# Expert-choice routing: the first expert's token numbers by four broadcast comparisons and one f16 number a token, with its gathers and its products moved forward in the written order

## The chip, the cores and the metric

One NeuronCore of one Trainium2 chip runs the whole program as one launch. It has five engines with a queue of instructions each: TensorE (PE, with its weight loads as PEld), VectorE (DVE), ScalarE (ACT), GpSimd (POOL) and SyncE (SP, which only issues DMAs here). An engine takes its instructions in the order of its queue; a wait holds all that stands behind it. The metric is the device time of one execution in microseconds; a profiled execution also gives a span, from the first to the last instruction.

## The reference

Three stages in f32, each on the output of the one before:

- Attention, 4 batches x 8 heads x 768 positions x 64: a position sees `n_sink` first positions and a window of `window` positions back; softmax; then the product with v.
- A dense layer on the 3072 x 512 result: `h = x @ w_in` (2048 wide), a smooth ReLU (0 below -1, (h+1)^2/4 between, h above 1), `@ w_out`.
- Expert choice among 8 experts of 384 places each:

```python
order = np.argsort(-flat)                      # all token x expert logits, largest first
for idx in order:
    tok, e = (int(idx) // E, int(idx) % E)
    if assigned[tok] >= 0 or counts[e] >= cap:
        continue
    assigned[tok] = e
    counts[e] += 1
...
for e in range(E):
    mask = assigned == e
    h = np.maximum(x[mask] @ w1[e], 0.0)       # 512 -> 1024
    out[mask] = h @ w2[e]                      # 1024 -> 512
```

## The kernel before, in words

Products are done in about f32 precision: each operand is split into a high and a low part ("h" and "l"), and a product is three matmuls, (low weights, high data), (high, low), (high, high).

The first 790 us hold attention and the dense layer, block by block of 256 tokens; the last block's logits are made before the rest of that block's output products (`up`, L663), so that the search for the first expert runs beside them. `logits` (L680) copies the logits from PSUM on ACT and turns them.

The routing is done expert by expert in the order in which experts fill up. `phase` (L789) holds the steps for one expert, the 3072 tokens lying as 128 partitions x 24 columns (GT = 24):

- `values`, `owners`: the best remaining logit of each token and its expert. Then seven rounds of a search for the threshold at which an expert is full: `compare` (DVE, 128 x 768), `count` and `total` (PE), `counts` and `bound` (DVE).
- `above`, `loads`, `choose`, `before`, `rank`: which expert is full, and the rank of each of its tokens (1 to 384). `choose` gives SP the expert's number for its weight loads.
- `places`: `a` (L943, L944), the place 1 to 128 of each token within a third of the expert's 384, and `rr` (L945), on POOL, which holds partition number and column number of a token, each in the column of its third.
- `slots(h)`, for h in 0 to 3: one-hot tiles `oh`, a comparison of the row 1 to 128 (`nrow`) with `a[:, t]` for each of the six columns t of a quarter: 24 DVE instructions of 128 x 128 in all (L958). `look(h)`: six matmuls with `oh` as weights and `rr` as data sum the numbers into `pk` in PSUM (L962). For the first expert a filler matmul (`unread`, L782), whose result nobody reads, follows each.
- `tokens`: ACT copies half of `pk` to SBUF (`tf`, L968), DVE makes 128 x column + partition of both halves, the token numbers `tok` (L972).
- `retire` (L926): five DVE operations that take the expert and its tokens out of the logits. The next expert's `values` need them.

`gather` (L1018) issues on POOL three indirect DMAs of 128 rows each by `tok` (L1025). `turn` (L1031): PE turns such a tile (`xt`, L1039), ACT copies it as the high part (`xsh`, L1040), DVE makes the low part (`xsl`, L1043). `expert` (L1047): for f = 0 to 7, `up` (12 matmuls into one of two PSUM buffers "H", which the fillers use as well), `act` (ACT) and `rest` (DVE, `hl`, L1076); from f = 3 on, `down` steps. `weight` (L977) brings the weights in eight pieces of 512 KB. A piece is loaded by SP into one of four buffers "er". For w2, and for the first piece of w1 of the first expert, ACT writes minus the weights (`minus`, L1000) and the high part (`lead`, L1006), and POOL issues a DMA that adds the weights to make the low part (`add`, L1010); for the other w1 pieces DVE makes the low part in two halves (`rest`, L1014). The first expert's other six pieces wait for its gathers (L992).

`experts` (L1121) writes all this into a plan: each step gets a time, and the steps of each engine are issued in the order of these times. `start` is the end of the logits. `T[k]` is the planned start of the products of expert k, `g` that of its three turns. The second expert's search is planned at `start + FIND + SECOND`, each later one at least `CHAIN` after the one before, and the T of each expert at least one of `PERIODS` after that of the one before. Steps given as `filler` are moved into planned gaps of DVE.

The planned times that the change touches, in us after `start`, before and after it:

| step (first expert, but for the search of the second) | before | after |
|---|---|---|
| `slots` 0 to 3 | 29.0, 29.6, 30.2, 30.8 | 29.0, 29.4, 29.8, 30.2 |
| `tokens` / `gather` / `retire` | 32.6 / 32.7 / 31.4 | 30.75 / 30.8 / 30.85 |
| `values` of the second search | 32.8 | 31.4 |
| `add` of the first w1 and the first w2 piece | 30.2, 40.8 | 31.8, 33.8 |
| `xt` 0 to 2 | 37.9, 39.2, 40.5 | 34.9, 36.23, 37.56 |
| `xsl` 0 to 2 | 39.35, 40.4, 42.15 | 36.1, 37.43, 38.76 |
| second search: `compare` 1, `count` 1, `total` 1 | 37.65, 38.65, 39.5 | 36.25, 37.25, 38.1 |
| second search: `bound` 1, `compare` 2, `count` 2 | 40.2, 41.1, 42.1 | 38.8, 39.7, 40.7 |
| loads of the other six weight pieces, from | 38.4 | 34.4 |
| T[0], first product | 42.8 | 38.8 |
| second low half of the second w1 piece / `compare` 3 | 46.25 / 44.55 | 44.2 / 43.15 |
| third part of the products of f = 1 / `up` f = 2, first part | 46.91 / 47.74 | 42.91 / 43.74 |
| third search: `count` 0 | 70.65 | 69.25 |
| T[1], T[2], T[3], T[4] | 82.3, 121.8, 161.3, 200.8 | 78.3, 117.8, 158.55, 198.05 |

Of the kernel before, what the change touches and what calls it, by code (L numbers as in the profile page):

```python
# [7 lines left out]
F32 = mybir.dt.float32  # L8
# [17 lines left out]
P = 128  # L26
# [33 lines left out]
SECOND, CHAIN, EARLY = 11.3, 34.8, 59.0  # L60
# [14 lines left out]
class Kernel:  # L75
# [547 lines left out]
    def moe1_steps(self, blk, xs, hold=None, part=None):  # L623
# [56 lines left out]
        def logits():  # L680
            lg = self.mo.tile([2 * E, TB], F32, name="lgs", tag="u")
            nc.scalar.copy(lg, st["lg"])
            ps = self.psum([P, 2, 2 * E], "A", "lt")
            for t in range(2):
                nc.tensor.transpose(ps[:, t], lg[:, t * P:(t + 1) * P], self.ident[:2 * E, :2 * E])
            o = self.logits[:, 2 * blk:2 * blk + 2, :]
            nc.vector.tensor_copy(o, ps[:, :, :E])
            nc.vector.tensor_tensor(out=o, in0=o, in1=ps[:, :, E:], op=OP.add)
# [47 lines left out]
    def pools2(self, e):  # L736
        tc = self.tc
        self.oh = e(tc.tile_pool(name="oh", bufs=1))
        self.ex = e(tc.tile_pool(name="ex", bufs=2))
        self.ew = e(tc.tile_pool(name="ew", bufs=2))  # L740

    def router_consts(self):
# [8 lines left out]
        self.nrow = rt.tile([P, P], BF16, name="nrow")  # L751
# [15 lines left out]
        self.t_row = rt.tile([P, GT], F32, name="t_row")  # L767
        nc.vector.tensor_copy(self.t_row, fl[:, 0, :GT])
# [20 lines left out]
    def phase(self, last, out, first=False):  # L789
# [147 lines left out]
        def places():  # L937
# [6 lines left out]
            nc.vector.scalar_tensor_tensor(a, a, -float(P), z, op0=OP.mult, op1=OP.add)  # L944
            rr = st["rr"] = self.rw.tile([P, GT, 2, 3], BF16, name="rr")  # L945

            nc.gpsimd.tensor_scalar(rr[:, :, 0].rearrange("p t c -> p c t"), bs, self.pcol, None, op0=OP.mult)
            nc.gpsimd.tensor_tensor(out=rr[:, :, 1].rearrange("p t c -> p c t"), in0=bs,
                                    in1=self.t_row.unsqueeze(1).to_broadcast([P, 3, GT]), op=OP.mult)
            st["oh"] = self.oh.tile([P, GT, P], BF16, name="oh", bufs=1)  # L950
            st["a"] = a
            st["pk"] = self.psum([P, 6], "A", "pk")
# [3 lines left out]
        def slots(h):  # L956
            for t in range(n_ * h, n_ * h + n_):
                nc.vector.tensor_scalar(st["oh"][:, t], self.nrow, st["a"][:, t:t + 1], None, op0=OP.is_equal)  # L958

        def look(h):  # L960
            for t in range(n_ * h, n_ * h + n_):
                nc.tensor.matmul(st["pk"], st["oh"][:, t], st["rr"][:, t].rearrange("p x c -> p (x c)"),  # L962
                                 start=(t == 0), stop=(t == GT - 1))
                if first and t < GT - 1:
                    self.unread(1, 5 * 32)
            if h == NQ - 1:
                st["tf"] = self.rw.tile([P, 3], F32, name="tf")
                nc.scalar.copy(st["tf"], st["pk"][:, 0:3])  # L968

        def tokens():  # L970
            out["tok"] = self.rw.tile([P, 3], I32, name="tok", bufs=3)
            nc.vector.scalar_tensor_tensor(out["tok"], st["pk"][:, 3:6], float(P), st["tf"], op0=OP.mult, op1=OP.add)  # L972
# [74 lines left out]
    def expert(self, cur):  # L1047
# [6 lines left out]
        def up(f):  # L1054
# [5 lines left out]
            def part(i):  # L1060
                w_, x_ = ((wl, xh), (wh, xl), (wh, xh))[i]
# [59 lines left out]
    def experts(self, plan, start):  # L1121
# [41 lines left out]
        for k in range(E):  # L1163
# [21 lines left out]
            if k == 0:  # L1185
                for dt, n in ((4.3, 10), (11.6, 8), (15.4, 4), (16.9, 2), (18.2, 2), (20.1, 3)):
# [4 lines left out]
            if k < 3:  # L1191

                for h in range(NQ):
                    at(t, ph["slots"], h)
                    at(t + 0.7, ph["look"], h)
                    t += 0.6
# [22 lines left out]
            for j in range(3):  # L1219
# [7 lines left out]
                filler(g + step * j + 1.2, 0.8, lambda tr=tr: tr["f"][1]())  # L1227
# [4 lines left out]
            for i, (c, name) in enumerate(PIECES):  # L1232
# [11 lines left out]
                if dma:  # L1244
# [3 lines left out]
                    at(a1 + 1.1 if k or i != 2 else T[0] - 2.0, add)  # L1248
# [5 lines left out]
            steps, ups, ends, act, rest = self.expert(cur)  # L1254
# [268 lines left out]
```

## Time and profile before

| | us |
|---|---|
| three timed runs | 1159.52 (median), 1156.93, 1160.38 |
| the profiled execution: its time, its span | 1156.74, 1154.9 |
| busy in the span: PE, PEld | 1101.7 (95%), 1014.5 (88%) |
| busy in the span: DVE, ACT, POOL | 872.7 (76%), 698.5 (60%), 487.2 (42%) |
| mean granted TensorE clock | 0.992 of 2.4 GHz |

A share of busy time is an average over stages. The stretch around the change lies between 814 us (end of the first search) and 835 us (first product of the first expert); from there to 1148 us the products of eight experts follow on PE. In a timeline each row is one or several like instructions: start, time from the start of the first to the end of the last, engine, line, operation, tiles, and in brackets how long the engine had been idle before it and what ended that.

### The profile page before, as it was taken

How to read it: one execution, taken by the hardware profiler on the slowest of the kernel's cores; microseconds unless marked ns; L12 is line 12 of the kernel's file. 1: busy time of each engine (PE TensorE's matmuls, PEld its weight loads, DVE VectorE, ACT ScalarE, POOL GpSimd, SP SyncE). 2: the span in 40 equal slices, each digit the busy share in tenths (PEclk: the TensorE clock that was granted, in tenths of full speed). 3: DMA queues.
4: the chain of work that ended last, by engine and by line, in shares of the span. 5: the costliest groups of instructions: out<-in, count | busy, mean ns of one | idle time of the engine just before them, and what ended most of it. 6: DMA issues, size and time to landing. Idle time of an engine off the chain costs nothing.

```text
span 1154.9 us, 24467 instructions
## 1 busy us (share of the span) xinstructions
PE 1101.7 (95%) x8308; PEld 1014.5 (88%) x8308; DVE 872.7 (76%) x2718; ACT 698.5 (60%) x1598; POOL 487.2 (42%) x590
## 2 busy tenths in 40 slices
PE   5899888999999999999999999999899999999997
PEld 3688878999999999999999999999678788888896
DVE  5978978777878878787878787755888888889430
ACT  4887777566777666776767676642245435444552
POOL 1335645445654545555545555541212323332321
PEclk9899999999999999999999999999999999999999
DMA  4645522222322223223222322000576767676872
GB/s 106 169 137 169 164 60 56 54 60 45 69 47 54 38 54 53 65 47 65 35 54 50 70 49 52 15 19 1 152 210 181 218 178 207 179 205 197 227 212 67
DMA packets 241928, 118.13 MB, mean 102 GB/s; under 512 B 196096, under 2 KB 220672, under 8 KB 241792
## 3 DMA queue, kind: packets, MB, share of 16 engines
q1 hardware_dynamic: 231504, 85.36, 28.7%
q0 software_dynamic: 8592, 29.89, 11.0%
q8 instruction: 67, 1.10, 0.4%
q10 hardware_dynamic: 1696, 1.22, 0.3%
q14 instruction: 69, 0.57, 0.2%
HBM read 86.00 MB, written 13.11 MB: 86 GB/s over the span
## 4 chain that ended last, share of the span: by engine, by line
PE 54%; DVE 13%; issue 7%; ACT 4%; POOL 3%; DMA 3%; SPq 1%; POOLq 0%; DVEq 0%; ACTq 0%
PE hp L638 17%; PE up L663 16%; PE us L1090 6%; PE hp L1063 6%; PE xp L391 3%; DVE ks L301 2%; PE tp L372 2%; PE sc L334 2%; PE sc L335 1%; DVE oh L958 1%; DVE ind L814 1%; DVE u L646 1%; PE pg L829 1%; DVE ql L317 1%; DVE w1l L1014 1%
## 5 line engine op out<-in xcount | busy, mean ns | idle before, releaser
L650 POOL TENSOR_TENSOR gl<-u,gh 128x256 fp32r<-128x256 f32 x192 | 153.2, 798 | 187.3 <-ACT gh L649 163.3
L663 PE MATMUL up<-woh,gl 128*128 128x256 f32 x576 | 166.5, 289 | 2.6 <-POOL gl L650 2.6
L663 PE MATMUL up<-woh,gh 128*128 128x256 f32 x576 | 163.8, 284 | 0.0
L663 PE MATMUL up<-wol,gh 128*128 128x256 f32 x576 | 163.5, 284 | 0.0
L647 ACT ACTIVATE u<-u,half 128x256 f32<-128x256 f32 x192 | 97.4, 508 | 79.3 <-DVE u L646 74.9
L638 PE MATMUL hp<-xh,wil 128*128 128x256 f32 x768 | 131.1, 290 | 4.0 <-ACT xh L411 3.2
L638 PE MATMUL hp<-xl,wih 128*128 128x256 f32 x768 | 125.8, 284 | 1.3 <-POOL xl L412 1.1
L638 PE MATMUL hp<-xh,wih 128*128 128x256 f32 x768 | 124.4, 283 | 0.0
L638 PEld LDWEIGHTS hp<-xh,wil 128*128 128x128 f32 x768 | 106.7, 190 | 5.9 <-ACT xh L411 4.3
L663 PEld LDWEIGHTS up<-woh,gl 128*128 128x128 f32 x576 | 108.9, 189 | 3.1 <-POOL gl L650 3.1
L663 PEld LDWEIGHTS up<-wol,gh 128*128 128x128 f32 x576 | 108.6, 188 | 0.4 <-issue 0.4
L663 PEld LDWEIGHTS up<-woh,gh 128*128 128x128 f32 x576 | 108.5, 188 | 0.4 <-issue 0.4
L638 PEld LDWEIGHTS hp<-xl,wih 128*128 128x128 f32 x768 | 106.1, 190 | 2.5 <-POOL xl L412 2.5
L638 PEld LDWEIGHTS hp<-xh,wih 128*128 128x128 f32 x768 | 106.1, 191 | 0.0
L646 DVE TENSOR_SCALAR u<-hp 128x256 f32<-128x256 f32 x192 | 80.1, 417 | 32.2 <-PE hp L638 24.4
L648 DVE TENSOR_TENSOR u<-hp,u 128x256 f32<-128x256 f32 x192 | 80.4, 419 | 31.4 <-ACT u L647 29.3
L649 ACT CAST gh<-u 128x256 fp32r<-128x256 f32 x192 | 77.5, 404 | 29.6 <-DVE u L648 26.9
L353 POOL TENSOR_TENSOR pr<-pr,sm 128x576 f32<-128x576 f32 x56 | 65.6, 1171 | 68.3 <-DVE ks L307 31.6
L339 ACT ACTIVATE pr<-pr,sm 128x288 f32<-128x288 f32 (+1 forms) x160 | 85.2, 533 | 12.6 <-DVE sm L337 11.7
L1071 ACT ACTIVATE hh<-hp 128x384 fp32r<-128x384 f32 x64 | 31.5, 492 | 100.6 <-PE hp L1063 86.4
L1090 PE MATMUL us<-w2h,hl 128*128 128x512 f32 x192 | 80.8, 421 | 0.0
L1090 PE MATMUL us<-w2h,hh 128*128 128x512 f32 x192 | 75.6, 394 | 0.0
(266 smaller groups left out, 3018.8 us busy)
## 6 DMA issues: line engine op xcount, KB each, us to landing
w1r<-in_moe_w_dram SPq DMA_DIRECT2D x32, 512.0 KB, 4.8
w2r<-in_moe_w_dram SPq DMA_DIRECT2D x32, 512.0 KB, 3.9
w2l<-w2r POOLq DMA_DIRECT2D x32, 512.0 KB
qr<-in_q_dram SPq DMA_DIRECT2D x320, 32.0 KB, 2.0
dr<-in_moe_w_in_dram SPq DMA_DIRECT2D x15, 512.0 KB, 3.9
dr<-in_moe_w_out_dram SPq DMA_DIRECT2D x15, 512.0 KB, 3.9
x2d<-ev SPq DMA_DIRECT2D x26, 256.0 KB, 2.5
vr<-in_v_dram SPq DMA_DIRECT2D x56, 96.0 KB, 2.4
```

Of the source, the lines that this page charges most:

```text
L339: nc.scalar.activation(pr, pr, AF.Exp, bias=sm[:, 0, u:u + 1], scale=-1.0, accum_out=sm[:, 1, u:u + 1])
L353: nc.gpsimd.tensor_tensor(out=pr, in0=pr, in1=r.unsqueeze(2).to_broadcast([P, 2, 2 * P + NS]), op=OP.mult)
L391: nc.tensor.matmul(o_, l, r, start=(i == 0), stop=(i == len(mm) - 1), skip_group_check=True)
L638: nc.tensor.matmul(ps, w_[:, k, fs], x_[:, k, :], start=(i == 0 and k == 0), stop=(i == 2 and k == 3))
L646: nc.vector.tensor_scalar(u, ps, -1.0, 1.0, op0=OP.max, op1=OP.min)
L647: nc.scalar.activation(u, u, AF.Square, bias=self.half, scale=0.5)
L648: nc.vector.tensor_tensor(out=u, in0=ps, in1=u, op=OP.max)
L649: nc.scalar.copy(gh, u)
L650: nc.gpsimd.tensor_tensor(out=gl, in0=u, in1=gh.bitcast(F32), op=OP.subtract)
L663: nc.tensor.matmul(o, g_[:, ts], self.w_out_part(w_, f)[:, cs], start=(f == fa and i == 0 and (cs.start > 0 or t == 0)), stop=(f == fz - 1 ...
L1063: nc.tensor.matmul(ps, w_[:, k, fs], x_[:, k, :], start=(i == 0 and k == 0), stop=(i == 2 and k == 3))
L1090: nc.tensor.matmul(us[j], h_[:, o], w_[:, f % 2, :], start=(f == 0 and i == 0), stop=(f == nf - 1 and i == 2))
```

## The change

Four things. First, for the first expert the one-hot tiles are made with the token column innermost: four DVE operations of 128 x 128 x 6, each comparing a stored f16 tile `slot` (the row 1 to 128 repeated 24 times, written once by four ACT copies queued behind the copy of the logits) with a broadcast of `a` in f16. The weights of `look` are then read from `oh` at a step of 24 elements. One filler of 512 columns follows each of the first three `look` steps, in place of 23 fillers of 160 columns. Second, for all experts `rr` holds one f16 number a token, its number minus 1536: one POOL operation in place of two, three result columns in place of six, no ACT copy, and `tokens` reads PSUM. Third, `tokens` and `gather` of the first expert come before `retire`, and the two DMAs that add weights behind the gathers. Fourth, the plan: times as in the table above, and the three parts of the first four `up` of the first expert in the order (high, high), (low, high), (high, low).

```diff
-SECOND, CHAIN, EARLY = 11.3, 34.8, 59.0
+SECOND, CHAIN, EARLY = 9.9, 34.8, 59.0
+XT, LEAD = 34.9, 38.8
...
-            nc.scalar.copy(lg, st["lg"])
+            self.copied = nc.scalar.copy(lg, st["lg"]).ins
...
+        self.slot = self.oh.tile([P, P, GT], F16, name="slot", bufs=1)
+        with tc.issue_after(self.copied):
+            for i in range(0, P, 32):
+                self.nc.scalar.copy(self.slot[:, i:i + 32],
+                                    self.nrow[:, i:i + 32].unsqueeze(2).to_broadcast([P, 32, GT]))
...
-        self.nrow = rt.tile([P, P], BF16, name="nrow")
+        self.nrow = rt.tile([P, P], F16, name="nrow")
...
-        self.t_row = rt.tile([P, GT], F32, name="t_row")
-        nc.vector.tensor_copy(self.t_row, fl[:, 0, :GT])
+        self.tok = rt.tile([P, GT], F32, name="tok_row")
+        nc.vector.tensor_scalar(self.tok, fl[:, 0, :GT], float(P), self.pcol, op0=OP.mult, op1=OP.add)
+        nc.vector.tensor_scalar(self.tok, self.tok, float(-N // 2), None, op0=OP.add)
...
-            rr = st["rr"] = self.rw.tile([P, GT, 2, 3], BF16, name="rr")
-
-            nc.gpsimd.tensor_scalar(rr[:, :, 0].rearrange("p t c -> p c t"), bs, self.pcol, None, op0=OP.mult)
-            nc.gpsimd.tensor_tensor(out=rr[:, :, 1].rearrange("p t c -> p c t"), in0=bs,
-                                    in1=self.t_row.unsqueeze(1).to_broadcast([P, 3, GT]), op=OP.mult)
-            st["oh"] = self.oh.tile([P, GT, P], BF16, name="oh", bufs=1)
-            st["a"] = a
-            st["pk"] = self.psum([P, 6], "A", "pk")
+            at = st["a"] = self.rw.tile([P, GT], F16, name="ah") if first else a
+            nc.vector.scalar_tensor_tensor(at, a, -float(P), z, op0=OP.mult, op1=OP.add)
+            rr = st["rr"] = self.rw.tile([P, GT, 3], F16, name="rr")
+            nc.gpsimd.tensor_tensor(out=rr.rearrange("p t c -> p c t"), in0=bs,
+                                    in1=self.tok.unsqueeze(1).to_broadcast([P, 3, GT]), op=OP.mult)
+            st["oh"] = self.oh.tile([P, P, GT] if first else [P, GT, P], F16, name="oh", bufs=1)
+            st["pk"] = self.psum([P, 3], "A", "pk")
...
+            ts = slice(n_ * h, n_ * h + n_)
+            if first:
+                nc.vector.tensor_tensor(out=st["oh"][:, :, ts], in0=self.slot[:, :, ts],
+                                        in1=st["a"][:, ts].unsqueeze(1).to_broadcast([P, P, n_]), op=OP.is_equal)
+                return
...
-                nc.tensor.matmul(st["pk"], st["oh"][:, t], st["rr"][:, t].rearrange("p x c -> p (x c)"),
+                nc.tensor.matmul(st["pk"], st["oh"][:, :, t] if first else st["oh"][:, t], st["rr"][:, t],
                                  start=(t == 0), stop=(t == GT - 1))
-                if first and t < GT - 1:
-                    self.unread(1, 5 * 32)
-            if h == NQ - 1:
-                st["tf"] = self.rw.tile([P, 3], F32, name="tf")
-                nc.scalar.copy(st["tf"], st["pk"][:, 0:3])
+            if first and h < NQ - 1:
+                self.unread(1)
...
-            nc.vector.scalar_tensor_tensor(out["tok"], st["pk"][:, 3:6], float(P), st["tf"], op0=OP.mult, op1=OP.add)
+            nc.vector.tensor_scalar(out["tok"], st["pk"], float(N // 2), None, op0=OP.add)
...
-                w_, x_ = ((wl, xh), (wh, xl), (wh, xh))[i]
+                w_, x_ = ((wl, xh), (wh, xl), (wh, xh))[(i + 2) % 3 if lead and f < 4 else i]
...
-                for dt, n in ((4.3, 10), (11.6, 8), (15.4, 4), (16.9, 2), (18.2, 2), (20.1, 3)):
+                for dt, n in ((4.3, 10), (9.4, 8), (13.1, 3), (14.5, 2), (15.0, 2), (16.8, 2)):
...
-                at(t, ph["retire"])
-                at(t + 1.2, ph["tokens"])
-                at(t + 1.3, self.gather, cur)
-                t += 1.3
-                g, step = t + 5.2, 1.3
-                T.append(max(T[-1] + PERIODS[k - 1], g + 4.9) if k else g + 4.9)
+                if k:
...
+                else:
+                    at(t + 0.15, ph["tokens"])
+                    at(t + 0.2, self.gather, cur)
+                    at(t + 0.25, ph["retire"])
+                    g, step = start + XT, 1.33
+                    T.append(start + LEAD)
...
-                filler(g + step * j + 1.2, 0.8, lambda tr=tr: tr["f"][1]())
+                if k:
+                    filler(g + step * j + 1.2, 0.8, lambda tr=tr: tr["f"][1]())
+                else:
+                    at(g + step * j + 1.2, lambda tr=tr: tr["f"][1]())
...
-                    at(a1 + 1.1 if k or i != 2 else T[0] - 2.0, add)
+                    at(a1 + 1.1 if k else max(a1 + 1.1, T[0] - 7.0 + i), add)
```

## Rows read from the trace of the kernel before

**Rows 1.** Busy by stage: stretch, length, each engine's busy time, PEclk, DMA share.

```profile
834.57:877.65 43.08, 41.60 (x293) 33.70 (x290) 36.52 (x143) 19.76 (x28) 9.99 (x11) 1.00 0.75 214
877.00:917.00 40.00, 39.35 (x279) 31.75 (x278) 33.74 (x135) 17.39 (x26) 9.15 (x12) 1.00 0.69 190
```

**Rows 2.** Timeline of PE: start, length, engine, line, operation, idle before.

```profile
829.90 0.63 PE L1039 MATMUL xt<-ident,xg 128*128 128x128 f32 x4 [1.01 <-issue]
...
832.43 0.63 PE L1039 MATMUL xt<-ident,xg 128*128 128x128 f32 x4 [0.27 <-DVE row L853]
...
834.57 0.94 PE L1063 MATMUL hp<-xsh,w1l 128*128 128x384 f32 x4
...
839.52 0.85 PE L1063 MATMUL hp<-xsh,w1l 128*128 128x384 f32 x4
840.22 0.86 PE L1063 MATMUL hp<-xsl,w1h 128*128 128x384 f32 x4
...
861.68 0.33 PE L962 MATMUL pk<-rr,oh 128*128 128x6 bf16 x6
```

**Rows 3.** Timeline of DVE.

```profile
820.20 4.38 DVE L958 TENSOR_SCALAR oh<-nrow,a 128x128 bf16<-128x128 bf16 x24
...
825.40 0.15 DVE L972 SCALAR_TENSOR_TENSOR tok<-pk,tf 128x3 int32<-128x3 f32 x1
...
829.55 0.96 DVE L814 TENSOR_TENSOR ind<-v,th 128x768 bf16<-128x768 f32 x1
...
840.40 0.96 DVE L814 TENSOR_TENSOR ind<-v,th 128x768 bf16<-128x768 f32 x1
```

**Rows 4.** Timeline of POOL.

```profile
823.76 1.13 POOL L1010 DMA_DIRECT2D w1l<-w1r  x1 [2.91 <-PE idle L787]
825.85 1.07 POOL L1025 DMA_INDIRECT xg<-x2d,tok  x1 [0.96 <-DVE tok L972]
...
828.51 0.95 POOL L1025 DMA_INDIRECT xg<-x2d,tok  x1 [0.30 <-issue]
829.47 1.04 POOL L1010 DMA_DIRECT2D w2l<-w2r  x1
```

**Rows 5.** Timeline of ACT.

```profile
817.24 0.37 ACT L710 COPY ev<-up 128x256 f32<-128x256 f32 x1 [24.74 <-PE up L663]
...
833.10 0.59 ACT L1040 CAST xsh<-xt 128x512 fp32r<-128x512 f32 x1 [0.84 <-PE xt L1039]
836.64 1.05 ACT L1006 CAST w1h<-w1r 128x1024 fp32r<-128x1024 f32 x1 [2.96 <-DMA w1r<-in_moe_w_dram]
```

**Rows 6.** Timeline of SP, which only issues DMAs.

```profile
832.49 1.12 SPq L991 DMA_DIRECT2D w1r<-in_moe_w_dram  x2
...
835.34 0.37 SPq L991 DMA_DIRECT2D w1r<-in_moe_w_dram  x1
```

**Rows 7.** DVE groups by form, 790 to 1155 us: count, busy us, mean ns of one.

```profile
L814 DVE TENSOR_TENSOR ind<-v,th 128x768 bf16<-128x768 f32 x35 | 33.5, 956 | 0.9
...
L877 DVE TENSOR_REDUCE ce<-w 128x8 bf16<-128x192 bf16 x8 | 4.0, 503 | 0.3
...
L804 DVE TENSOR_TENSOR own<-logits,v 128x192 bf16<-128x192 f32 x8 | 2.8, 352 | 0.1
...
L895 DVE TENSOR_TENSOR w<-own,est 128x192 bf16<-128x192 bf16 x8 | 2.1, 258 | 0.0
```

**Rows 8.** Weight loads of PE by form, the whole run: count, busy us, mean ns.

```profile
L1063 PEld LDWEIGHTS hp<-xsh,w1h 128*128 128x128 f32 x256 | 43.8, 188 | 0.1
L372 PEld LDWEIGHTS tp<-ident,pr 128*128 128x128 f32 x296 | 41.6, 207 | 3.7 <-POOL pr L353 3.5
...
L962 PEld LDWEIGHTS <-oh 128*128 128x128 bf16 x192 | 9.3, 96 | 8.5 <-DVE oh L958 3.2 <-issue 1.8 <-PE idle L787 1.0
```

**Rows 9.** Busy by stage, early in the attention.

```profile
28.00:32.00 4.00, 2.30 (x15) 1.64 (x13) 3.77 (x17) 3.92 (x13) 2.60 (x5) 1.00 0.27 52
32.00:44.00 12.00, 11.50 (x51) 9.28 (x52) 11.77 (x39) 8.88 (x26) 5.47 (x9) 0.72 0.61 163
```

More of the change, by code (lines that the diff above doesn't have):

```diff
@@ L943, in places @@
             nc.vector.tensor_tensor(out=a, in0=ge[:, 1], in1=ge[:, 2], op=OP.add)
-            nc.vector.scalar_tensor_tensor(a, a, -float(P), z, op0=OP.mult, op1=OP.add)
-            rr = st["rr"] = self.rw.tile([P, GT, 2, 3], BF16, name="rr")
-            nc.gpsimd.tensor_scalar(rr[:, :, 0].rearrange("p t c -> p c t"), bs, self.pcol, None, op0=OP.mult)
-            nc.gpsimd.tensor_tensor(out=rr[:, :, 1].rearrange("p t c -> p c t"), in0=bs,
-                                    in1=self.t_row.unsqueeze(1).to_broadcast([P, 3, GT]), op=OP.mult)
-            st["oh"] = self.oh.tile([P, GT, P], BF16, name="oh", bufs=1)
-            st["a"] = a
-            st["pk"] = self.psum([P, 6], "A", "pk")
+            at = st["a"] = self.rw.tile([P, GT], F16, name="ah") if first else a
[5 more added lines that the diff above has]
+            st["pk"] = self.psum([P, 3], "A", "pk")
         n_ = GT // NQ
         def slots(h):
-            for t in range(n_ * h, n_ * h + n_):
+            ts = slice(n_ * h, n_ * h + n_)
[3 more added lines that the diff above has]
+                return
+            for t in range(ts.start, ts.stop):
                 nc.vector.tensor_scalar(st["oh"][:, t], self.nrow, st["a"][:, t:t + 1], None, op0=OP.is_equal)
@@ L1045, in turn, with expert @@
         return turned, rest
-    def expert(self, cur):
+    def expert(self, cur, lead):
         nc, a, tc = self.nc, self.a, self.tc
@@ L1194, in experts @@
                     at(t, ph["slots"], h)
-                    at(t + 0.7, ph["look"], h)
-                    t += 0.6
-                at(t, ph["retire"])
-                at(t + 1.2, ph["tokens"])
-                at(t + 1.3, self.gather, cur)
-                t += 1.3
-                g, step = t + 5.2, 1.3
-                T.append(max(T[-1] + PERIODS[k - 1], g + 4.9) if k else g + 4.9)
+                    at(t + (0.7 if k else 0.5), ph["look"], h)
+                    t += 0.6 if k else 0.4
+                if k:
+                    at(t, ph["retire"])
+                    at(t + 1.2, ph["tokens"])
+                    at(t + 1.3, self.gather, cur)
+                    t += 1.3
+                    g, step = t + 5.2, 1.3
+                    T.append(max(T[-1] + PERIODS[k - 1], g + 4.9))
+                else:
[4 more added lines that the diff above has]
+                    T.append(start + LEAD)
                 if T[k] - 6.2 > g:
@@ L1252, in experts @@
                         filler(a1 + 1.2 + 0.7 * u, 2.5, rest, u)
-            steps, ups, ends, act, rest = self.expert(cur)
+            steps, ups, ends, act, rest = self.expert(cur, k == 0)
             d = PERIODS[k] / len(steps)
```

## The prediction

> **What bounds the kernel now.** I read the stages first, to see which engine sets the time behind the change. From the first product of the first expert (834.57 us) to that of the second (877.65 us) PE is busy 41.60 of 43.08 us, and 39.35 of 40.00 us in the next stage [rows 1]. So behind 834.57 us PE is the bound, and a product that starts earlier carries through to the end, as long as nothing that PE waits for stays where it was. Ahead of it PE waits for one chain, read from the timelines of the engines: DVE makes 24 one-hot tiles from 820.20 to 824.58, the token numbers come at 825.40, after the logits' update [rows 3], POOL issues gathers from 825.85 to 829.46 [rows 4], PE turns the tiles from 829.90 to 832.43 and starts products at 834.57 [rows 2]. Last I read, for the weights of the first expert, SP [rows 6] and ACT [rows 5]: their loads leave at 832.49, behind the last gather, and the cast of the second w1 piece runs at 836.64.
>
> **The one-hot tiles.** Removed: 24 operations, 4.38 us. Added: four of 128 x 768 with 16-bit operands; none stands in the trace. With an f32 operand the same size takes 956 ns, and 192 elements take 352, so an element costs (956 - 352) / 576 = 1.05 ns. With 16-bit operands alone 192 elements take 258, 94 less, which is about half of 192 x 1.05: half an element's time is saved [rows 7]. For 768 that gives 956 - 400 = 556 ns. Here the elements come in rows of six with a hop between; a reduction that hops at each of 192 elements takes 503, 151 more than the operation of 352, or 0.8 ns a hop [rows 7], so 128 hops add 0.1: 0.66. In a queue the next one starts before the last is out; I take 0.56 a piece and 0.66 for the last: 820.2 + 3 x 0.56 + 0.66 = 822.5. Ends: 0.46 a piece, 822.1; at full length (0.87 a piece), 823.8.
>
> **The look-up and the numbers.** Six matmuls of the last quarter follow. With contiguous weights six took 0.33 [rows 2]; I take 0.43, because the weights now lie 48 bytes apart. The ACT copy and the logits' update no longer stand in between, so DVE makes the numbers at 822.5 + 0.43 = 822.95, against 825.40: 2.45 earlier. The lower end is 0.33. The upper end: a 16-bit load takes 96 ns, an f32 load 188, and an f32 load in steps of two 207 [rows 8]; at 0.207 each, six take 1.24, four such quarters with three fillers (about 0.2 each) become longer than the DVE work, and the numbers come at 820.7 + 4 x 1.24 + 0.7 = 826.4. The nearest row by type is the 96. Against it speaks a rule of the Trainium skill (Advanced Engine Details and Errata, Memory Cachelines): full rate needs two hits on a 16-byte line, and here each column is on a line of its own. No run here shows 16-bit weights so spaced; the same skill (TensorE: Matmul & The Clock Gate, Weight-path perf modes) lets the fast weight load read strided columns, which would leave 0.33.
>
> `rr` as one POOL operation, and the missing ACT copy, cost or save nothing: POOL and ACT are idle there, and `rr` is used only after the first one-hot. The ACT fill of `slot`, four copies of 768 elements, is some 3.4 us by the 1.05 of 1024 [rows 5]; ACT is idle for 24.74 us before 817.24 [rows 5], which hides it. Without that cover (fill behind the copies at 817.24) the tiles would start at about 822, 1.7 later.
>
> **The gathers.** POOL starts 0.30 after the numbers (825.55 to 825.85): 823.4. The third starts 2.66 behind the first (825.85 to 828.51) [rows 4]: 826.05. The first tile landed 4.05 after its start (829.90) and the third 3.95 after (turned at 832.43, SP free at 832.49) [rows 2, 6]: now 827.45 and 830.0. The DMA that adds to w1 stood ahead of the gathers at 823.76 [rows 4] and now stands behind; a quicker landing by that I leave to the range.
>
> **Turns and the first product.** The update now follows the numbers and takes about 1 us (824.58 to 825.40 is its visible part), so the second search starts near 824.2, 1.3 earlier; its `compare` 1, at 829.55 before, could run at 828.2. But in the new order `xsl` 0 stands ahead of it on DVE and waits for the first tile: turned at 827.45, cast 0.67 later for 0.59 (832.43 to 833.10 and on) [rows 2, 5], 828.7; `xsl` of 512 elements by 352 + 320 x 1.05 is 0.69, of which 0.6 blocks DVE: 829.3. `compare` 1 ends at 830.25, `count` 1 takes 0.15, and behind it on PE stands the third turn: 830.4. Its tile is cast at 830.4 + 0.67 + 0.59 = 831.65, and the first product, which with the new order of parts needs only the high halves, starts there: 2.9 earlier than 834.57. The plan's 4.0 is not reached.
>
> **What is late next.** (a) The second part needs the first w1 piece's low half. Its adding DMA is now issued after the third gather, 827.0. How long one takes is read from the w2 one: issued at 829.47, and SP's load at 835.34, which reuses the buffer that it reads, waits for it: 5.9 [rows 4, 6]. It is there at 832.9, and the part wants it at 832.35: 0.5 lost, 0 to 2.6 for a DMA of 4 to 8 us. (b) The loads behind the gathers go at 830.0, not 832.49; the second w1 piece is cast 4.15 after (832.49 to 836.64) for 1.05: 835.2. From there DVE took until 840.40, 2.7 us after the cast's end at 837.69, for a low half, `hl` 0, the other low half and a `bound`, and then began `compare` 4 [rows 3, 5]. The new order puts a `compare`, 0.96, in between before the second half is made: 835.2 + 2.7 + 0.96 = 838.85. The products of f = 2 need both halves from their second part on, which ran at 840.22 [rows 2]. So there the gain is down to 1.4. Below, it would be nothing if the weights came no earlier; above, 2.9 if DVE kept ahead.
>
> **Until the second expert.** PE idles 43.08 - 41.60 = 1.48 us in this stage [rows 1], at `count` steps that come before DVE is ready. Products stand 4.0 earlier in the plan and the search 1.4, so each count comes 2.6 later behind the products; I take 1.0 of the 1.48 as regained (ends 0 and 1.48). At the second expert the gain is 2.4. After it PE idles 0.65 in 40 us, the third search starts no earlier than before, and the plan gives T[3] only 2.75 of the 4.0: I take off 0.3 (0 to 1.0). Forecast: 2.1 us less.
>
> **The sum.** 1156.74 for the profiled execution less 2.1 is 1154.6. That execution is 0.2 below the fastest of the three timed ones; all four have a mean of 1158.4, which I use as the level: 1156.3.
>
> **Rivals.**
> - Most of the shift passes: one-hot pieces at 0.46, tiles landing 0.5 sooner without the adding DMA ahead, DVE ahead of the products. The product starts at 830.9, no loss at f = 2, and the plan's 2.75 at T[3] with the lost waits gives 3.2 to 3.7: 1155.0. For it: DVE idle while the tiles fly. Against: the weights leave only after the gathers.
> - Weight loads at the 48-byte step are slow. From 0.17 us a load on, four quarters are longer than the old chain to 825.40; at 0.207 the numbers come 1.0 later than before, everything behind moves with them, and the earlier counts return nothing: slower, 1159.5. For it: the 207 row. Against: that row's loads move four-byte elements, whose contiguous load is 188 already. The rule of the Trainium skill on lines (Memory Cachelines, above) is this case's mechanism.
> - The clock falls. After a stretch in which PE was busy 2.30 of 4.00 us the granted clock was 0.72 on average over 12 us, between 2.4 and 1.2 GHz: 0.28 x 12 = 3.4 us of work lost [rows 9]. Fillers here are rearranged, and by my times PE is busy some 60% from 823 to 831.6. If the products start at 1.2 GHz: 1156.3 + 3.4 = 1159.7. Against it: the stage that follows ran at 1.00 before [rows 1] with waits as long.
> - It doesn't do what it says: `slot` is filled late, or the adding DMA takes 8 us; 1.7 or 2.1 of the gain are lost: 1158.2.
>
> **How the numbers follow.** Forecast 0.45; most passes 0.20; slow loads 0.10; clock 0.08; late fill or late DMA 0.17. The forecast's own range, by its bounds and a level uncertain by 1.5, is 1154.3 to 1158.3. The range over the cases is 1152.7 to 1159.9. A measurement of this kernel tells 0.3%, 3.5 us, from no change. Faster by more needs the second case and luck, or the first with much luck: 0.27. Slower by more needs slow loads or the clock and something else: 0.09. Within: 0.64.
>
> **What would show it.** Right: four DVE rows `oh` of some 0.65 us, ending by 822.6; the numbers before 823.2; the third turn held by `count` 1, not by its tile; the first product near 831.7; PE idle ahead of the second part, and again at f = 2 for a `w1l`; the second expert's first product about 2.4 earlier. Wrong: `oh` rows of 0.9, `pk` steps longer than the `oh` rows, PEclk under 1.00 from 825 on, or a PE stall at the `count` 0 of the third or fourth search that takes the gain back.

## The result, and the profile after: slower by 0.8%

The changed kernel takes 1167.58 us (median of 6 runs, 1163.96 to 1168.64), the kernel before in the same comparison 1158.35 (6 runs, 1156.44 to 1160.38): ratio 1.0076, 95% interval 1.0065 to 1.0088. I forecast 1156.3 in a range up to 1159.9. The profiled execution took 1167.97 us (span 1166.2), 11.23 more than the one before. Of that 1.07 had arisen ahead of anything that the change touches: the copy of the last block's logits, `lgs`, starts at 793.20 us instead of 792.13. Runs of kernels that are the same up to there differ by as much (791.5 to 794.2), so below I count from that copy.

Busy by stage, from the first product of one expert to that of the next, as in [rows 1] (stretch, length, busy time and count of PE, PEld, DVE, ACT, POOL, then PEclk, DMA share, GB/s):

```profile
834.17:882.64 48.47, 44.56 (x287) 35.94 (x288) 37.31 (x143) 18.11 (x26) 7.31 (x8) 0.93 0.70 195
882.64:924.88 42.24, 41.38 (x292) 33.58 (x291) 35.52 (x140) 20.34 (x28) 12.50 (x13) 1.00 0.75 198
924.88:967.89 43.01, 40.61 (x293) 33.49 (x290) 35.37 (x143) 18.04 (x27) 10.71 (x11) 1.00 0.67 180
967.89:1011.59 43.70, 42.63 (x277) 35.25 (x278) 34.40 (x136) 18.52 (x26) 10.50 (x11) 0.92 0.69 183
```

The second to fourth of these stages in the kernel before:

```profile
877.65:919.41 41.76, 41.11 (x293) 33.22 (x290) 35.36 (x141) 18.61 (x28) 10.49 (x12) 1.00 0.70 191
919.41:959.68 40.27, 39.92 (x287) 32.80 (x284) 34.27 (x139) 17.79 (x28) 10.87 (x12) 1.00 0.65 188
959.68:1000.27 40.59, 39.88 (x279) 33.05 (x278) 34.09 (x133) 19.09 (x28) 12.15 (x13) 1.00 0.75 203
```

The first product is 1.47 us earlier, but the first stage takes 48.47 us instead of 43.08, the second 42.24 instead of 41.76, the third 43.01 instead of 40.27 and the fourth 43.70 instead of 40.59; the rest is the same to 0.1. -1.47 + 5.39 + 0.48 + 2.74 + 3.11 = 10.25. The granted clock is below 1.00 in two of the stages; of the six runs the fastest, 1163.96 us, has the highest mean clock, 0.990, the others 0.984 or 0.985. The first three rows here are stretches around the first products of the first expert, the last one lies behind the fourth expert's first product:

```profile
830.00:834.00 4.00, 4.00 (x25) 2.15 (x23) 2.39 (x5) 1.64 (x3) 1.42 (x2) 0.63 0.94 206
838.00:842.00 4.00, 1.38 (x9) 1.06 (x8) 1.22 (x4) 2.29 (x3) 0.00 (x0) 1.00 1.08 392
842.00:850.00 8.00, 7.15 (x37) 6.12 (x37) 6.25 (x20) 3.81 (x6) 0.84 (x1) 0.58 0.74 173
970.00:985.00 15.00, 15.00 (x83) 13.05 (x83) 10.65 (x46) 6.67 (x9) 1.21 (x2) 0.79 0.63 169
```

The timelines (start, length, engine, line, operation; in brackets idle before and what ended it). DVE, to set beside [rows 3]:

```profile
821.48 2.12 DVE L964 TENSOR_TENSOR oh<-slot,ah 128x768 f16<-128x768 f16 x4
824.56 0.16 DVE L979 TENSOR_SCALAR tok<-pk 128x3 int32<-128x3 f32 x1 [0.95 <-PE pk L972]
825.78 0.35 DVE L804 TENSOR_REDUCE v<-logits 128x24 f32<-128x192 f32 x1
840.78 0.69 DVE L1021 TENSOR_TENSOR w1l<-w1r,w1h 128x512 fp32r<-128x512 f32 x1 [3.57 <-ACT w1h L1013]
841.39 0.55 DVE L1083 SCALAR_TENSOR_TENSOR hl<-hp,hh 128x384 fp32r<-128x384 f32 x1
```

PE, beside [rows 2], and last the weight loads of the first expert's look-up from 820 to 825 (count, busy us, mean ns), beside the contiguous ones of [rows 8]:

```profile
824.00 0.52 PE L972 MATMUL pk<-rr,oh 128*128 128x3 f16 x6
829.33 0.87 PE L1046 MATMUL xt<-ident,xg 128*128 128x128 f32 x4 [0.39 <-issue]
834.17 0.96 PE L1070 MATMUL hp<-xsh,w1h 128*128 128x384 f32 x4
842.00 0.98 PE L1070 MATMUL hp<-xsh,w1h 128*128 128x384 f32 x4 [2.62 <-DVE hl L1083]
845.75 1.63 PE L1070 MATMUL hp<-xsl,w1h 128*128 128x384 f32 x4
953.75 0.30 PE L972 MATMUL pk<-rr,oh 128*128 128x3 f16 x6
967.89 0.97 PE L1070 MATMUL hp<-xsh,w1l 128*128 128x384 f32 x4 [0.68 <-ACT xsh L1047]
...
L972 PEld LDWEIGHTS <-oh 128*128 128x128 f16 x24 | 2.1, 169 | 1.3 <-PE idle L794 1.1
```

POOL, SP and ACT, beside [rows 4 to 6]:

```profile
825.69 1.16 POOL L1032 DMA_INDIRECT xg<-x2d,tok  x1 [4.35 <-DVE logits L941]
829.49 1.02 POOL L1017 DMA_DIRECT2D w1l<-w1r  x1
830.12 1.30 POOL L1017 DMA_DIRECT2D w2l<-w2r  x1
832.38 1.86 SPq L998 DMA_DIRECT2D w1r<-in_moe_w_dram  x2
839.71 1.04 ACT L1013 CAST w1h<-w1r 128x1024 fp32r<-128x1024 f32 x1 [5.59 <-DMA w1r<-in_moe_w_dram]
```

The reader should follow the last two: the second w1 piece, loaded from 832.38, is cast at 839.71, 7.33 us later; before it was 4.15 [rows 5, 6]. DVE waits 3.57 us for it, with `hl` queued behind, and PE 2.62 us for `hl`. After that idle time PE's groups of four take 1.63 us instead of 0.86: the clock is granted at the lower of its two levels, 1.2 instead of 2.4 GHz, for most of 842 to 850.

### The profile page after: what moved, and what is told of

Read it like the earlier page. It is cut to its first block, busy times and chain, and to the rows that moved or that the text cites. A ratio compares the mean times of both kernels' runs of the same rounds, so it can differ in the third digit from the quotient of the medians.

```text
span 1166.2 us, 24388 instructions
## 1 busy us (share of the span) xinstructions
PE 1109.7 (95%) x8286; PEld 1019.7 (87%) x8286; DVE 871.0 (75%) x2699; ACT 700.4 (60%) x1594; POOL 481.3 (41%) x582
## 4 chain that ended last, share of the span: by engine, by line
PE 54%; DVE 13%; issue 7%; ACT 4%; DMA 3%; POOL 3%; SPq 1%; POOLq 0%; ACTq 0%; DVEq 0%
PE hp L639 15%; PE up L664 14%; PE hp L1070 8%; PE us L1097 7%; PE xp L392 2%; PE tp L373 2%; DVE ks L302 2%; PE sc L335 1%; PE sc L336 1%; SPq L427 1%; DVE u L647 1%; DVE ind L821 1%; DVE ql L318 1%; DVE w1l L1021 1%; DVE oh L968 1%
## 5 line engine op out<-in xcount | busy, mean ns | idle before, releaser
L1017 POOL DMA_DIRECT2D w2l<-w2r x32 | 29.6, 925 | 114.4 <-ACT w2l L1007 106.2
```

## The experiments

All runs in one table: time, ratio to the kernel before in the same comparison with its interval, and the first products of experts 1 to 5 and 8 in us behind `lgs`, worked out from the timelines (good to 0.01). Each ratio is against the kernel before as it ran beside that version, so a median of one row is not to be set against that of another.

| run | us | ratio | 1 | 2 | 3 | 4 | 5 | 8 |
|---|---|---|---|---|---|---|---|---|
| before | 1158.35 | | 42.44 | 85.52 | 127.28 | 167.55 | 208.14 | 322.99 |
| after | 1167.58 | 1.0076 [1.0065, 1.0088] | 40.97 | 89.44 | 131.68 | 174.69 | 218.39 | 333.16 |
| e1 | 1164.68 | 1.0056 [1.0039, 1.0073] | 43.39 | 86.49 | 128.69 | 171.70 | 214.14 | 328.91 |
| e2 | 1164.49 | 1.0057 [1.0040, 1.0074] | 41.07 | 89.86 | 132.12 | 176.17 | 216.41 | 331.20 |
| e3 | 1159.38 | 1.0012 [1.0003, 1.0022] | 43.83 | 86.63 | 128.36 | 169.12 | 209.79 | 324.58 |
| e4 | 1162.45 | 1.0039 [1.0025, 1.0053] | 43.38 | 86.42 | 128.63 | 172.68 | 212.92 | 327.70 |
| e5 | 1157.62 | 1.0001 [0.9988, 1.0014] | 42.71 | 85.48 | 127.28 | 167.94 | 208.56 | 323.37 |
| e6 | 1161.52 | 1.0031 [1.0018, 1.0045] | 42.46 | 85.53 | 127.77 | 171.81 | 212.06 | 326.85 |
| e7 | 1159.82 | 1.0019 [1.0008, 1.0030] | 43.11 | 87.41 | 129.61 | 170.28 | 210.93 | 325.72 |
| e8 | 1160.03 | 1.0027 [1.0014, 1.0041] | 43.64 | 87.77 | 129.96 | 170.78 | 211.40 | 326.22 |
| e11 | 1163.20 | 1.0042 [1.0028, 1.0056] | 41.02 | 86.15 | 128.37 | 171.40 | 215.10 | 329.88 |
| e9 | 1157.80 | 0.9997 [0.9988, 1.0006] | 42.27 | 85.08 | 127.36 | 167.62 | 208.26 | 323.03 |
| e13 | 1156.77 | 0.9988 [0.9980, 0.9997] | 41.79 | 84.82 | 127.03 | 167.30 | 207.97 | 322.74 |
| e12 | 1159.17 | 1.0009 [0.9996, 1.0021] | 42.51 | 85.96 | 127.96 | 168.24 | 208.88 | 323.65 |
| e14 | 1157.48 | 0.9994 [0.9985, 1.0003] | 41.79 | 84.79 | 127.05 | 167.32 | 207.93 | 322.72 |

**e1, the w1 adding DMA ahead of the gathers again.**

```diff
-at(a1 + 1.1 if k else max(a1 + 1.1, T[0] - 7.0 + i), add)
+at(a1 + 1.1 if k or i != 2 else T[0] - 5.0, add)
```

> The changed kernel with one step put back: the DMA that adds the first w1 piece stands ahead of the gathers on POOL again (planned 30.2, was 31.8). Theory A (the adding DMA, moved behind the gathers, shares the DMA engines with the loads of the second w1 piece, which then land 7.3 us after their issue instead of 4.2; DVE, then PE wait for them, and PE's clock falls after the wait): the cast of the second w1 piece comes about 2 us earlier, the 2.6 us wait of PE at f = 2 goes below 0.6, the first expert takes 4 to 5 us less, and the time is about 1163.5. Theory B (the rearranged fillers let PE's clock fall, and that is the loss by itself): the cast moves, but the clock still falls around 830 and 844; 1166. Theory C (one-hot tiles read at a step of 48 bytes cost PE time): no change, 1167.5.

The second w1 piece is cast 3.66 us behind its load (834.50 to 838.16), the stall at the third group is gone, and the first stage takes 43.10 us, as before: for cast and stall theory A holds. But the first tile is late again, and the first product 2.4 later than in the changed kernel. The clock still fell ahead of it (0.64 from 830 to 834, 0.51 from 834 to 838), and the time lies between the 1163.5 of A and the 1166 of B. The third expert's stage stays at 43.0.

**e2, the fourth expert's products not held back in the plan.**

```diff
-T.append(max(T[-1] + PERIODS[k - 1], s + 7.0 + 6.2))
+T.append(T[-1] + PERIODS[k - 1] if k == 3 else max(T[-1] + PERIODS[k - 1], s + 7.0 + 6.2))
```

> The changed kernel with T[3] planned at T[2] + 39.5 (157.3 instead of 158.55), without the clause that puts it 13.2 us behind the fourth expert's tokens. Theory A (the plan leaves the turns of expert 3 exposed behind the last products of expert 2; PE idles 2.5 us there and its clock then falls for some 7 us): the third and fourth expert start 40 to 40.5 us after the one before as in the kernel before, no clock under 1.00 around 970 us, and 5 us less: 1162.5. Theory B (the waits there come from the second and third search being late on DVE, whatever the plan says): the products then wait for the gathers or the casts instead, 1166 to 1168. Theory C: no change, 1167.5.

The stage of the third expert grows to 44.05 us, so it wasn't the plan's clause that cost time there; PE now waits 0.98 us for the gathered rows at the first turn, as theory B had it. The next stage is 40.24 with the clock at 1.00, against 43.70: the clock's fall near 970 in the changed kernel (PE busy 10.51 of 13.00 us from 957 to 970, against 11.60 here) costs some 3.

```profile
970.00:985.00 15.00, 15.00 (x87) 13.31 (x87) 12.43 (x59) 9.04 (x12) 3.21 (x5) 1.00 0.70 208
```

**e3, the quick numbers alone**: one-hot tiles, look-up and one number a token as changed; plan, order of the update, adding DMA and order of parts as before.

> The new one-hot tiles, f16 numbers and the fill of the stored tile alone; the written order, the fillers and every planned time are those of the kernel before (update ahead of the token numbers, first products at 42.8, order of the three parts as before). Theory A (the loss is all in the moved plan): the gathers start about 1 us earlier than before, held then by the stores of the last block's rows; no loss behind; 1157.3 beside 1158.4 of the kernel before. Theory C (the new tiles themselves are the loss): 1165 or more. Theory B (fillers: those of the look-up are new here too, the rest are old): no clock fall, 1158.

1.4 us slower than before, which none of the three theories had. The numbers come 1.9 us earlier, the first tile does not, and PE has nothing in between:

```profile
825.70 1.02 PE L794 MATMUL idle<-one 128*128 128x512 bf16 x4
829.86 1.08 PE L1046 MATMUL xt<-ident,xg 128*128 128x128 f32 x4 [3.14 <-issue]
```

```profile
830.00:834.00 4.00, 4.00 (x24) 2.85 (x25) 1.76 (x8) 1.17 (x2) 0.19 (x1) 0.50 0.97 213
```

After 3.14 us without work the clock is 0.50, and from the first turn to the first product it takes 5.87 us instead of 4.67 [rows 2].

**e4, e1 and e2 together.**

> Both edits: the first w1 piece's adding DMA ahead of the gathers, and T[3] at T[2] + 39.5. Theory A (two losses, each with its own place): the two gains add, 1167.5 - 4.5 - 5 = 1158, and what is left of the earlier first product shows as 0 to 2 us less than the kernel before. Theory B: 1165. If only one of the two places was a cause, the time is that of the run with that edit alone.

The two gains do not add to the 1158 of theory A: 1162.45. What is left is 0.9 at the second expert, with a clock of 0.50 from 830 to 834, and 3.8 in the stage of the third.

**e5 and e6, more fillers ahead of the first turn**, in e3 and in e4:

```diff
-(15.4, 4)                 # e3
+(15.4, 17)                # e5
-(9.4, 8), (13.1, 3)       # e4
+(9.4, 12), (13.1, 13)     # e6
```

> The quick numbers alone in the old plan (as in the run of the numbers alone), with 17 instead of 4 filler matmuls ahead of the first turn. Without them PE was idle 3.14 us there, the granted clock fell to 0.50, and from the first turn to the first product it took 5.87 us instead of 4.67. Theory, the clock: with PE kept busy the granted clock stays at 1.00 from 826 to 836, that stretch takes 4.7 us again, and the kernel is 1.2 us faster than the numbers alone, about 0.2 us above the kernel before. Rival, the tile itself is late or DVE holds the turn: the clock may stay up, but the time moves by less than 0.4 us. Other side: the fillers hold PE beyond the tile's landing, first turn after 830.2, and the time is above that of the numbers alone.

> The changed kernel with the w1 adding DMA ahead of the gathers and the fourth expert's products not held back in the plan, and 25 instead of 11 fillers between the look-up and the first turn. Theory: two separate losses were left, the clock from 828 to 836 (1.1 us) and the stage of the third expert (44.05 us instead of 40.27). The fillers take only the first: clock 1.00, first product 1.1 us earlier, third expert's stage still 43.5 to 44.3, and the time is 1.1 us less than without fillers, some 3.4 us above the kernel before. Rival, the clock is what makes that stage long as well: the whole 4.5 us goes.

As the theory has it: e5 has the clock at 1.00 in that stretch,

```profile
830.00:834.00 4.00, 3.51 (x29) 1.97 (x28) 1.16 (x7) 1.17 (x2) 1.87 (x2) 1.00 0.81 240
```

first turn to first product takes 4.67 us, and the loss of e3 is gone. e6 gains 0.9 and keeps the third stage at 44.04: that one is not the clock.

**e7, an equal shift**: turns and products 1.4 us earlier than before, as the searches, instead of 4.0; the adding DMA as in e1. **e8**: e7 with the fillers of e6.

```diff
-XT, LEAD = 34.9, 38.8
+XT, LEAD = 36.5, 41.4
```

> The changed kernel with the w1 adding DMA ahead of the gathers, and turns and products of the first expert planned 1.4 us earlier than in the kernel before, as much as the searches, instead of 4.0. Theory: the third expert's stage took 44 us because the products were planned 2.6 us further ahead than the searches, so that the fourth expert's rows are gathered too late for them. With equal shifts that stage is back at 40.2 to 40.8 us, the later ones at 40.0, and what remains is the clock ahead of the first product: 0.5 to 1.5 us above the kernel before. Rival, something in the new look-up or the new order of parts makes the stage long: it stays at 43 to 44 us and the time at 4 to 5 us above.

> The equal shift with 25 instead of 11 fillers ahead of the first turn. Theory: clock at 1.00 from 826 on, third expert's stage 40.2 to 40.8 us, and nothing is left of the loss: 0 to 1.0 us below the kernel before, the gain limited by the tiles, which land no earlier than before behind the adding DMA. Rival, the clock ahead of the first product is hidden by the searches later: no difference to the equal shift without fillers.

The third stage is back at 40.67 and 40.82 us. e7 differs from e1 in the shift alone, and there the stage took 43.01: its length came from products planned 2.6 further ahead than the searches. How it shows depends on the clause of e2. Without it (e4) the fourth expert's gather starts 33.2 us behind the third expert's first product, and PE waits for the rows; in e7 it starts 29.1 behind. With the clause (e1 and the changed kernel) the turns are planned later, and PE waits around them for the search and for the casts, as in the row at 967.89 above. First e4, then e7, the gather and the turn:

```profile
953.52 1.07 POOL L1032 DMA_INDIRECT xg<-x2d,tok  x1 [14.48 <-DVE cnt L842]
957.53 0.66 PE L1046 MATMUL xt<-ident,xg 128*128 128x128 f32 x4 [0.99 <-DMA xg<-x2d,tok]
```

```profile
951.80 1.07 POOL L1032 DMA_INDIRECT xg<-x2d,tok  x1 [11.30 <-issue]
957.13 0.66 PE L1046 MATMUL xt<-ident,xg 128*128 128x128 f32 x4 [0.23 <-DMA xg<-x2d,tok]
```

The time of e7, some 2 us above the kernel before, is a little beyond the 0.5 to 1.5 expected. For the time of e8 I was wrong. The fillers filled the one wait that I had seen; PE then waited 0.97 us for a `cnt` and 1.54 for an `ind`, at counts that the plan puts between the turns, and the clock fell there:

```profile
834.00:838.00 4.00, 2.49 (x16) 2.19 (x17) 2.72 (x9) 1.63 (x2) 0.00 (x0) 0.69 1.04 356
```

**e11, the changed kernel with the first w1 piece's low half made by DVE**, so that no w1 adding DMA is there; the w2 one stays 5.0 ahead of the planned first product.

```diff
-dma = name == "w2" or (first and c == 0)
+dma = name == "w2"
+at(start + 32.75 + 1.1 * u, rest, u)     # for the first piece
```

> The changed kernel, but the low half of the first w1 piece is made by DVE (two subtractions of 0.68 us, behind the owners and behind the first counts of the second search), so that no w1 adding DMA stands behind the gathers; the w2 one stays. Theory, the adding DMAs behind the gathers slow the loads: half of their bytes go, so the second w1 piece is cast 5 to 6 us behind its load instead of 7.3, the stall of 2.62 us ahead of the third group of products shrinks to 1 or less, the clock stays up from 842 to 850, and the time is 2 to 4 us below the changed kernel. Rival, the loads are slow because they are issued behind late gathers, whatever else flies: cast 7 us behind the load as before, time the same. Either way the third expert's stage stays long (above 42.5 us).

```profile
830.85 1.09 SPq L998 DMA_DIRECT2D w1r<-in_moe_w_dram  x2
835.14 1.05 ACT L1013 CAST w1h<-w1r 128x1024 fp32r<-128x1024 f32 x1 [2.65 <-DMA w1r<-in_moe_w_dram]
...
840.00:848.00 8.00, 7.45 (x41) 6.27 (x41) 6.49 (x21) 3.19 (x6) 0.66 (x2) 0.79 0.74 198
```

4.29 us from load to cast, behind gathers exactly as late as in the changed kernel: the adding DMA made the load slow, not its issue. By the ratios 3.9 us of the loss are gone, by the trace 3.3 at the eighth expert, within the 2 to 4 expected. But the clock did not stay up as the theory had it: it fell behind two waits for the search (0.77 us for an `ind`, 0.56 for a `cnt`) and was 0.79 from 840 to 848. The first stage is 45.13 us, not yet the 43.08 of before. The third stays long (43.02), as both theories had it.

**e9, together**: e11's low half, the equal shift, the w2 adding DMA planned 0.5 behind the first product, fillers spread over the waits between the turns (`(9.4, 12), (13.1, 3), (14.5, 2), (15.0, 2), (16.5, 4), (17.8, 5)`). **e13**: e9 with the update ahead of the numbers again:

```diff
-at(t + 0.25, ph["retire"])
+at(t, ph["retire"])
```

> What the runs so far point to, together: equal shift of 1.4 us for searches, turns and products; gathers first on POOL; low half of the first w1 piece on DVE; the w2 adding DMA only 0.5 us behind the planned first product, behind the loads; fillers spread over the waits between the turns. Theory: the first tile lands 3.6 us behind its gather and 1.6 us earlier than behind an adding DMA, the first product is 41 us behind the logits' copy (before 42.4), the first stage takes 43.0 to 43.6 us, the third 40.2 to 40.8, clock 1.00 throughout, and the time is 0.5 to 1.6 us below the kernel before. Rival, the searches alone set the later experts: with 0.7 us more on DVE ahead of them all but 0.7 us of the shift is gone at the fourth expert, 0 to 0.5 us below. Other side: a clock fall or a late second w1 piece as before, 1 to 2 us above.

> As the run with the equal shift and the low half on DVE, but on DVE the logits' update stands ahead of the token numbers again, as in the kernel before. Theory: DVE waits 0.95 us for the look-up anyway and the update takes about that, so the numbers come as early as with the gathers' order (31.4 us behind the logits' copy in both), and the second search starts 1.0 to 1.1 us earlier. The first product hangs on that search (it stands behind count 2 on PE, which waited 0.86 us for DVE), so it comes 0.7 to 1.1 us earlier, the fourth expert's too, and the time is 0.4 to 1.1 us below that run. Rival, the tiles or the weights set the first product: it moves by less than 0.3 us and the time not at all.

e9 has the clock at 1.00 throughout and lands at the time before, no better: the rival, the searches, held. The later planned place of the w2 adding DMA changed nothing, since POOL has no other work in between: it still went right behind the third gather and ahead of the loads (832.35), whose second w1 piece was cast 4.96 us behind them.

```profile
829.54 1.03 POOL L1017 DMA_DIRECT2D w2l<-w2r  x1
```

In e13 the numbers come as early and the search 1.1 us earlier. DVE in e9, then in e13:

```profile
824.58 0.16 DVE L979 TENSOR_SCALAR tok<-pk 128x3 int32<-128x3 f32 x1 [0.96 <-PE pk L972]
825.81 0.35 DVE L804 TENSOR_REDUCE v<-logits 128x24 f32<-128x192 f32 x1
```

```profile
824.15 0.16 DVE L979 TENSOR_SCALAR tok<-pk 128x3 int32<-128x3 f32 x1
824.27 0.35 DVE L804 TENSOR_REDUCE v<-logits 128x24 f32<-128x192 f32 x1
```

From `lgs` (793.22 and 792.82) that is 31.36 and 31.33 for the numbers, 32.59 and 31.45 for the values. The update fits into the 0.96 us that DVE waits for the look-up anyway. The first product came 0.48 earlier, less than the 0.7 expected; it still stands behind count 2, which waits for DVE:

```profile
834.45 0.31 PE L836 MATMUL pg<-own,ind 128*128 128x32 bf16 x6 [0.68 <-DVE ind L821]
834.61 0.96 PE L1070 MATMUL hp<-xsh,w1h 128*128 128x384 f32 x4
```

e13 is the one version whose interval lies below the kernel before. By its trace it is worth 0.25 us at the last expert; the ratio gives 1.4, with an interval that nearly touches none. e14 below, whose products stand within 0.04 us of those of e13, has an interval that contains 1, so a gain is not shown beyond doubt.

**e12, the same with the low half made by POOL and everything planned 2.0 earlier.**

> The same with the low half of the first w1 piece made by POOL behind the gathers instead of by DVE, and searches, turns and products planned 2.0 us earlier than in the kernel before instead of 1.4. Theory: the search no longer pays for the low half, first product 40.2 to 41.0 us behind the logits' copy (before 42.4), fourth expert's first product 165.6 to 166.6 (before 167.55), clock 1.00, time 0.8 to 1.8 us below the kernel before: the whole of what the quick one-hot tiles can give. Rival, something off the search (the w1 low half on POOL late, the second w1 piece, the clock) takes it: not below the run with DVE.

The rival came, by a way that I had not thought of. `compare` 1 runs 0.8 us earlier than in e13 (35.47 against 36.29 behind `lgs`), but then the search stands still. DVE, and below it POOL:

```profile
829.67 0.96 DVE L821 TENSOR_TENSOR ind<-v,th 128x768 bf16<-128x768 f32 x1
830.55 2.58 DVE L828 TENSOR_TENSOR part<-pat,th 128x32 int32<-128x32 int32 x1
833.05 0.68 DVE L1050 TENSOR_TENSOR xsl<-xt,xsh 128x512 fp32r<-128x512 f32 x1
```

```profile
830.57 2.50 POOL L1021 TENSOR_TENSOR w1l<-w1r,w1h 128x512 fp32r<-128x512 f32 x2
```

`part`, an operation of 0.18 us elsewhere, takes 2.58, until POOL's two subtractions are over. So moving work to POOL took DVE's time all the same. The Trainium skill (SBUF — State Buffer, Terms) says that DVE and POOL share a pair of ports, that an instruction holds it for its whole length and that the other engine fully blocks; these rows agree.

**e14, e13 with a small DMA on POOL ahead of the first gather.**

> As the run with the update first, with one small DMA (128 x 24 numbers, read by nobody) issued by POOL between its product `rr` and the first gather. In six traces in which the gather is POOL's first DMA after a long pause it starts 0.97 to 0.98 us behind the token numbers; in the kernel before, with the adding DMA ahead of it, 0.30. Theory: the first DMA after the pause pays the 0.67 us, whatever it is, so the gather now starts 0.30 behind the numbers, 0.67 earlier. Rival, the wait belongs to something else the gather needs (the rows' stores landing, the buffers): it still starts 0.97 behind. For the time I expect within 0.7 us of the run without it in either case, since the first product stands behind count 2, which waits for DVE and not for the tiles.

```profile
821.14 0.78 POOL L1027 DMA_DIRECT2D small<-tok_row  x1
825.54 1.24 POOL L1036 DMA_INDIRECT xg<-x2d,tok  x1 [3.62 <-DVE v L804]
```

The numbers were ready at 824.58, so the gather started 0.96 behind them all the same. My theory of a cost of the first DMA falls; what the wait belongs to stays open.

## Why the prediction was wrong

- **One-hot tiles and look-up: right in kind, the look-up's end mis-sized.** Four operations took 0.53 us each, 0.56 forecast. The numbers came 1.91 us earlier behind `lgs` (31.36 against 33.27), 2.45 forecast: DVE stood 0.95 for the last quarter, where I had counted 0.43. The first operation also began 0.21 later (28.28 behind `lgs` against 28.07), 0.15 of it because `ah`, begun behind `rr` on POOL, took 0.33 us where `a` had taken 0.18 (for the third expert of e12, where it begins ahead of `rr`, it takes 0.18 again): that `rr` costs nothing was not quite so. Six look-ups at the 48-byte step took 0.52 us, six contiguous ones 0.30 in the same trace. Their loads took 169 ns each on average, contiguous ones 96, so the rival of slow loads was right about the single load; but the loads overlap, one about every 0.07 us, where the rival had put them one behind the other. A quarter with its filler took 0.59 us on PE and 0.53 on DVE, and the rival did not come. (The rule of the Trainium skill, Advanced Engine Details and Errata, Memory Cachelines, that accesses each on another line cost, agrees in direction; it gives no size.)
- **"POOL starts 0.30 after the numbers": 0.97.** The gathers gained 1.23, not 2.45.
- **The first product** came 1.47 earlier instead of 2.9. Of the difference of 1.43, 0.54 is the look-up and 0.67 the start of the gather; the tile came 0.41 sooner behind its gather than counted (3.64 against 4.05), no adding DMA being ahead of it; and 0.64 was lost from the first turn to the first product (4.84 against 4.20), where the clock was 0.63 from 830 to 834.
- **"Loads go at 830.0", "cast 4.15 after": the step that failed.** They went 1.2 earlier behind `lgs` instead of 2.5 (832.38 less 793.20 against 832.49 less 792.13), and the cast came 7.33 after. I had priced the moved adding DMA by when its own result is there (0.5 us), and had moved the loads' duration over unchanged from a trace in which that DMA was over before they began. In the changed kernel two adding DMAs of 512 KB run when the loads start. e11 takes one away, and the cast is 4.29 behind the loads again, the stall of 2.62 gone.
- **The clock: a rival given 0.08, and it decided.** It fell three times. Ahead of the second and the third fall the change had left PE emptier: busy 1.38 of 4.00 us from 838 to 842, where the kernel before, as far behind `lgs`, has no gap, and 11.53 of the 13.00 us ahead of the fourth expert's first product (13.00 before). Ahead of the first it had not clearly (2.15 of the 4.00 us up to the first turn, 2.09 before), so why that one came is not shown. By the rows of the result the missing clock is worth 0.37 x 4, 0.42 x 8 and 0.21 x 15 us of PE's work, an estimate of 8.0 beside the 10.25 lost in all. e5 shows that fillers take such a first fall away (1.2 us in e3, whose PE was busy 0.86 of 4.00 from 826 to 830). I had looked only at the stretch up to 831.6 and not at what the stall at f = 2 would do.
- **"I take off 0.3" at the fourth expert: 2.7, and 3.1 behind it.** I had read the plan's 2.75 as a gain given; the searches, only 0.8 us earlier (values 32.58 behind `lgs` against 33.39; 1.3 forecast), could not follow. e7 against e1 shows it: with equal shifts the stage is 40.67 again instead of 43.01. The 3.1 behind it is the clock's third fall, which e2 does not have.
- The forecast's base, that an earlier first product carries to the end, needed the search to come along. With most of these losses mended (e9; its second stage still takes 42.28 us, against 41.76) the kernel is at 0.9997 of before: PE is busy, but its order holds a count of the search ahead of the products, and DVE sets when that is ready.

## What to carry to other kernels

When a DMA is moved, price what flies beside it at its new place, not only when its result is there: every load's duration in the old trace belongs to the old neighbours. When products are moved ahead of a chain that shares the engine's order with them, the chain has to move as far, or the wait comes back some stages later. And when work in a gap is made shorter, read the granted clock behind the gap: a filler is part of the time.

## What the hardware showed that I had not expected

- A DVE operation of 0.18 us took 2.58 beside subtractions on POOL (e12).
- Two adding DMAs of 512 KB in flight stretch the time from a weight load's issue to its cast to 7.33 us (7.70 in e2), against 3.6 to 5.0 with one (before 4.15, e1 3.66, e11 4.29, e9 4.96).
- Behind an adding DMA on POOL the first tile is turned 6.4 to 6.5 us after that DMA's start with the gather 1.4 behind it (e3: 823.43 to 829.86; e4: 823.24 to 829.67; e1: 825.46 to 831.97), and 6.1 after it with the gather 2.1 behind (before: 823.76 to 829.90): an earlier gather brings no earlier tile. Without it the turn comes 3.6 to 3.8 after the gather's start (changed kernel: 825.69 to 829.33; e13: 825.28 to 829.11).
- The first expert's first gather starts 0.96 to 0.98 us behind the token numbers in seven traces without that adding DMA ahead, the second expert's 0.27 to 0.28, the fourth's 0.8 in both kernels and 0.27 to 0.29 in e2 and e4. It is not a pause of POOL (gathers after 8.3 us of idle time start 0.28 behind their numbers) and not the first DMA (e14). The last row stores had landed by 1.0 to 1.2 us before the gather; whether it waits for them in some other way stays open.
